# Rows scattered into the experts' lists when a block is routed, and plain loads of them in the second MoE

## The chip, the cores and the metric

The kernel runs on one core of one Trainium2 chip, as one program. Its five engines have their own instruction queues: PE (TensorE, matrix products; PEld is its weight load), DVE (VectorE), ACT (ScalarE), POOL (GpSimd) and SP (SyncE), which here only issues DMAs. The metric is the device time of one execution in microseconds (us); smaller is better. All times are of the same inputs.

## The reference

Three layers follow one another: attention over a window of 64 keys (4 batches, 8 heads, 576 positions, head size 64), a gated MLP with an RMS norm ("first MoE", 2304 tokens, 512 to 1536 to 512), and a mixture of 8 experts ("second MoE") in which each token goes to one expert:

```python
xn = x / sqrt(mean(x * x) + 1e-6) * rms_g            # first MoE
x2 = (silu(xn @ w_gate) * (xn @ w_val)) @ w_out      # (2304, 512)

logits = x2 @ wg2                                    # second MoE, 8 experts
e = argmax(logits); gw = softmax(logits)[e]
out[t] = gw[t] * (relu(x2[t] @ w1[e]) @ w2[e])       # 512 -> 1024 -> 512
```

## The kernel before, in words

The order of instructions on each engine is the order of the Python code (a manual schedule). DMAs issued by SP are plain; those issued by POOL are indirect: 128 rows go to, or come from, the DRAM rows that 128 indices name.

**First MoE.** The tokens are worked off in four blocks of 768, 768, 384 and 384 tokens, and a block of 768 in two parts of 384. A unit is one part with one of 12 slices of the hidden size; there are 72 units (loop at line 808). In a unit PE does the gate and value products (`gate_val`, line 560), ACT and DVE the activation (`silu`: a tanh on ACT at line 576, then DVE's lines 577, 578 and 580), and PE adds the output product of the unit before (`out_b`, line 597). After a part's last unit `evac` (line 603) copies its rows from PSUM into tiles `x2` and SP writes them to the DRAM tensor `x2dram` (line 614). Some work is put beside the units by a budget of VectorE time (`beside`, line 270): the norms of parts that come later (`norm`, line 308, which loads the attention's rows into a tile `xr` and squares them on ACT at line 328), the weights' conversion, and `route`.

**Routing.** `route(n)` (line 621) computes for a block's tokens the logits, the expert, the gate weight and the place `posi` in the expert's list. At line 697 POOL scatters, for each tile of 128 tokens, the pair (token number, gate weight) to row `posi` of `table` in DRAM; a memset (line 696) stands between two scatters. The last block is routed in `tail` (line 882), during the first item of the second MoE.

**Second MoE.** It has 9 items: expert 0's first 2 tiles of tokens, expert 0's next 2 tiles, then up to 4 tiles of each of the experts 1 to 7. Item 0 takes only tokens of the first two blocks, so that its list is ready early. `c_gather(i)` (line 748) loads an item's rows of `table` into a tile `ix` by SP (line 754, after all scatters so far have landed) and then gathers the tokens' rows from `x2dram` by POOL, tile by tile (line 759), into `xr` (even items) or `sq` (odd items). `c_transpose` (line 762) brings them on PE into the layout of the products, 128 tokens at a time (line 769). An item has 8 steps. The weights of all items stream through a ring of 18 places (`c_load`, line 736). `c_out` (line 938) scales an item's rows and scatters them into the output by POOL (line 944). List places that no token fills hold token number 2304, whose row of `x2dram` is zero; and when item 0 gathers, the rows of later blocks may be addressed too, so line 841 fills them from that zero row.

Lists beyond 4 tiles take a loop at the end that still reads `x2dram`; it has no turns with these inputs.

Of the kernel before, what the change touches and what calls it, by code (L numbers as in the profile page):

```python
# [23 lines left out]
E = 8  # L24
# [5 lines left out]
TINY64 = 3.4332275390625e-05  # the high word of 2.0 ** -126 as a float64, read as float32  # L30
# [3 lines left out]
# tokens of the first MoE: blocks that share a pass over the weights, in parts that share a product  # L34
BLOCKS = [[384, 384], [384, 384], [384], [384]]
SUB = 384
NXT = 3  # parts whose normed tokens are held
LEAD = 2  # steps by which the second part comes after the first at the start
MF = 1  # the last block whose tokens the second MoE's first item takes

# attention: groups of 3 query blocks from scores to transposes, to products with the values
LT, LV = 4, 5
NQK = 3  # pairs of heads whose queries and keys are held
G_LOAD, G_CONV, G_NORM = 8, 14, (12 + LV, 25 + LV)  # groups with which other work begins
CREDIT = 0.3, 0.8  # VectorE's time in us for other work beside a group: before, after the second norm's begin
BUDGET = [4.8, 3.4, 4.2, 4.2]  # the same beside a part's step, for each block
# [3 lines left out]
def attention_moe_moe_kernel(ctx, tc, qT, kT, vw, w1p, rms_g, wg2, wg2T, w2p, out):  # L50
# [13 lines left out]
    for i in range(2):  # L64
        # what the first MoE's products don't reach
        nc.vector.memset(bank[i][:, SUB:], 0.0)
# [17 lines left out]
    # places handed out so far, per partition: summed over the partitions, expert e's start at e * NT  # L84
# [4 lines left out]
    x2dram = dram.tile([NT + 1, DM], F32, name="x2dram")  # L89
    table = dram.tile([E * NT, 2], I32, name="table")  # L90
# [3 lines left out]
    # the second MoE takes over the first one's tiles  # L94
# [6 lines left out]
    # as many words are 2 steps of the first MoE and 3 of the second  # L101
# [6 lines left out]
    def xt_views(at, n):  # L108
        """Both parts of [P, 4, n] from word at on."""
        return [xt_t[:, a:a + 4 * n].rearrange("p (c t) -> p c t", c=4) for a in (at, at + 4 * n)]  # L110
# [12 lines left out]
    def parts_tiles(pl, key, n, w):  # L123
        """Places for n steps' weights in two parts, with what they hold and the step that needs it last."""
        return [[pl.tile([P, w], F32R, name=f"w{x}{key}{i}") for x in "hl"] + [None, i - n] for i in range(n)]
# [4 lines left out]
    def place(k, key, what):  # L130
        """Step k's place for the parts of what, and whether they are there."""
        p = next((p for p in places[key] if p[2] == what), None)
        here = p is not None
        if not here:
            p = min(places[key], key=lambda p: p[3])
        p[2:] = what, k
        wh_t[k, key], wl_t[k, key] = p[:2]
        return here

    # ------------------------------------------------------------------ attention  # L140
    actx = ExitStack()
    f_p = pool("fill", 1, actx)
    # additive masks on the raw scores, rows (head, query), columns keys of the window
# [17 lines left out]
    # queries of a pair of heads, [row in its block, block]; each head's rows are 0 in the other's columns  # L161
# [9 lines left out]
    def qk_load(u):  # L171
        if u < NU:
            b, hp = divmod(u, NHP)
            k_t[u] = a_q.tile([P, S], F32, name="kt")
            q_t[u] = qz[u % NQK]
            for h in range(2):
                r = slice(64 * h, 64 * h + 64)
                nc.sync.dma_start(q_t[u][r, r], qT[b, hp, r])
            # what the first scores need comes first
            cuts = [0, 192, S] if u == 0 else [0, S]  # L180
            for c in (slice(*x) for x in zip(cuts, cuts[1:])):
                nc.sync.dma_start(k_t[u][:, c], kT[b, hp, :, c])
# [66 lines left out]
    # ------------------------------------------------------------------ work beside PE's  # L249
    class Task:  # L250
        """A generator of small pieces of work. After each it gives what the piece cost VectorE in us,
        "bank" where it needs a PSUM bank until its next yield, "rest" where it would wait for another engine,
        or "step" where it would wait for longer."""
# [16 lines left out]
    def beside(tasks, budget):  # L270
        """Pieces of the tasks, the first ones first, as many as the budget allows."""
# [14 lines left out]
    def on_bank(tasks, bk):  # L286
        """The piece of the first task that asks for a bank."""
# [5 lines left out]
    # ------------------------------------------------------------------ norm of the attention's output  # L293
    # blocks of tokens that share a pass over the weights, in parts that share a product
# [13 lines left out]
    def norm(i):  # L308
        t0, nt, _ = subs[i]
        if i == 1:  # L310
            # in the place of weights that come later
# [37 lines left out]
        for _ in range(NEWTON):  # L349
            # y (the root times sc) -> y * (y * y * m / sc^2 - 3), the root times -2 * sc  # L350
# [21 lines left out]
    # ------------------------------------------------------------------ weights of the first MoE  # L372
# [3 lines left out]
    def w_load(i):  # L376
        """The i-th half of a step's weights."""
# [9 lines left out]
    def w_conv(f):  # L387
        """float64 words -> float32: sign and top exponent bit, low exponent bits and mantissa;
        what is under float32's normal range becomes 0."""
# [38 lines left out]
    # ------------------------------------------------------------------ run: attention  # L428
# [24 lines left out]
    def early_splits():  # L453
        """The first step's weights in parts."""
# [59 lines left out]
    # ------------------------------------------------------------------ first MoE  # L514
# [3 lines left out]
    def w_split(k, what, src, w_in, eng, parts="ao"):  # L518
        """Parts of float32 weights that one pass each carries: [P, w_in] for the first product(s), [P, 512]
        for the last. The second parts are left to the caller: what each costs VectorE in us, and its call."""  # L520
# [16 lines left out]
    # there and back, so that the parts at hand serve the next block too  # L537
    steps = [(n, f, list(blocks[n][2])) for n in range(len(blocks)) for f in range(NF)[::-1 if n % 2 else 1]]
    # the second part of the tokens starts later
# [43 lines left out]
    def last_mm(w, h, banks, f0, f1):  # L583
        """Adds a step's part to the output of token tiles."""
# [36 lines left out]
    def route(n):  # L621
        """Expert, weight and place in the expert's list for the tokens of block n."""
# [14 lines left out]
        if not last:  # L637
            lg = small("lg")
            for j, x2 in enumerate(x2_t.pop(n)):
# [5 lines left out]
        else:  # L645
            # on PE, in banks that nothing else needs then
# [15 lines left out]
        # the first of the largest  # L662
# [29 lines left out]
        before, now = scat[-1:], []  # L692
        for j in range(T):
            if j > 0:
                # two neighbours in an engine's order can't be declared independent
                nc.gpsimd.memset(apart, 0.0)
            d = nc.gpsimd.indirect_dma_start(out=table[:, :], in_=ent[:, j], in_offset=None,
                                             out_offset=bass.IndirectOffsetOnAxis(ap=posi[:, j], axis=0)).ins
            for o in now:
                tc.declare_no_dep(d, o, reason="other rows; the readers wait for all")  # L700
            for o in before[-1] if j == 0 and before else []:
                after(d, o)
            now.append(d)
# [12 lines left out]
    # ------------------------------------------------------------------ second MoE: parts  # L716
# [4 lines left out]
    # lists of token tiles of an expert: first expert 0's first tiles, kept to the first blocks' tokens,  # L721
    # which needn't wait for the others' routing
# [25 lines left out]
    def c_gather(i):  # L748
        if i >= len(items):
            return  # L750
        e, t0, T = items[i]
        ix = ix_t[i] = i_p.tile([P, 4, 2], I32, name="ix")
        rows = table[e * NT + t0 * P:e * NT + (t0 + T) * P]
        d = nc.sync.dma_start(ix[:, :T], rows.rearrange("(j p) w -> p j w", p=P)).ins
        for o in scat[-1]:
            after(d, o)
        xg = xg_t[i] = big(i % 2)
        for j in range(T):
            nc.gpsimd.indirect_dma_start(out=xg[:, j, :DM], out_offset=None, in_=x2dram[:, :],
                                         in_offset=bass.IndirectOffsetOnAxis(ap=ix[:, j, 0:1], axis=0))  # L760
# [13 lines left out]
    # places that expert 0's list leaves free in its first tiles  # L774
# [20 lines left out]
    # ------------------------------------------------------------------ run: first MoE  # L795
# [20 lines left out]
    for u, (k, i) in enumerate(units):  # L816
# [8 lines left out]
        # one that is free until the next step's second product  # L825
# [12 lines left out]
        if begin and n == MF:  # L838
            # rows that the first gather doesn't need, but addresses
            done = blocks[MF + 1][0]  # L840
            nc.sync.dma_start(x2dram[done:NT], x2dram[NT:NT + 1].to_broadcast([NT - done, DM]))
# [14 lines left out]
        if n == len(blocks) - 1 and last:  # L856
            # the second MoE's weights, where nothing reads the first one's any more
# [13 lines left out]
    # ------------------------------------------------------------------ second MoE  # L871
# [10 lines left out]
    def tail():  # L882
        """What follows the last block's output, up to the first list of its tokens."""
# [10 lines left out]
    def cases(i, body, unit=P // 2):  # L894
        """body(number of tokens), run by PE alone: not fewer than item i has, but for those beyond its tiles."""
# [57 lines left out]
    def over_slots():  # L953
        # what an expert has beyond 4 tiles goes into slots of 2 tiles: their expert and first table row
# [29 lines left out]
        # unused slots: within bounds  # L984
# [133 lines left out]
```

## Time and profile before

| what | us |
|---|---|
| three runs | 913.20, 912.89, 916.03 (median 913.2) |
| profiled execution, span from first to last instruction | 911.7 |
| PE busy | 852.8 (94%) |
| DVE busy | 674.6 (74%) |
| POOL busy | 253.4 (28%) |
| HBM traffic | 87.1 MB read, 19.6 MB written |

The profiled execution has no other time than its span; the median of the runs lies 1.5 us above it. Attention ends at about 135 us, the first MoE at about 621 us, and the second MoE takes the rest. In the chain of work that ended last PE has 53% of the span, DVE 26% and DMA 6%.

A row of the timeline gives the start, the duration, the engine, the line, the operation and the tiles (out<-in); in square brackets stands how long the engine was idle before it and what it waited for. A granted clock (PEclk) of 1.00 is 2.4 GHz and 0.50 is 1.2 GHz.

### The profile page before, as it was taken

The page shows a single profiled execution, that of the slowest core. Times are in us where ns is not written, and L with a number is a line of the kernel's source. Part 1 is how long each engine was busy: PE and PEld are TensorE (multiplying, and loading weights), DVE is VectorE, ACT ScalarE, POOL GpSimd, SP SyncE. Part 2 cuts the span into 40 slices and gives each one's busy share as a digit, 9 for nine tenths or more (in the row PEclk, how much of TensorE's full clock was granted, in tenths as well). Part 3 has the DMA queues.
Part 4 walks back from the last instruction along what each step waited for, and adds up shares of the span by engine and source line. Part 5 has one row for each costly group of instructions (what it writes and reads, how often), then busy time and mean ns, then how long its engine had stood idle before and what let it go on. Part 6 is the DMA issues. An engine that isn't in the chain of part 4 may idle for free.

```text
span 911.7 us, 13573 instructions
## 1 busy us (share of the span) xinstructions
PE 852.8 (94%) x4667; PEld 777.7 (85%) x4667; DVE 674.6 (74%) x1535; ACT 415.3 (46%) x951; POOL 253.4 (28%) x268
## 2 busy tenths in 40 slices
PE   8999988999999999999999899999799999899994
PEld 8999977878888999999998889888688888788883
DVE  7779989999997677776588974986485656566462
ACT  5777764334443433322333324334364545565351
POOL 3337753224323000000302243233312330333021
PEclk9999989999999999999999999999899999899998
DMA  7887623343332421000010004423376664663010
GB/s 213 286 269 241 196 86 129 104 139 104 97 112 93 139 35 35 1 1 1 17 54 1 1 1 165 171 93 83 116 215 194 210 210 122 219 209 94 3 44 17
DMA packets 40896, 102.96 MB, mean 113 GB/s; under 512 B 10576, under 2 KB 15056, under 8 KB 40659
## 3 DMA queue, kind: packets, MB, share of 16 engines
q1 hardware_dynamic: 35090, 88.29, 30.6%
q0 software_dynamic: 5696, 13.14, 5.0%
q8 instruction: 78, 1.28, 0.6%
q14 instruction: 32, 0.25, 0.1%
HBM read 87.08 MB, written 19.57 MB: 117 GB/s over the span
## 4 chain that ended last, share of the span: by engine, by line
PE 53%; DVE 26%; issue 8%; DMA 6%; ACT 4%; POOL 3%; SPq 0%; another core or an unknown queue 0%; DVEq 0%; POOLq 0%; ACTq 0%
PE bank L56 50%; DVE junk L642 6%; DMA out_dram<-x,ix 3%; DVE wla L529 3%; DVE wraw L408 2%; DVE wraw L405 2%; DVE wraw L415 2%; DVE t L578 2%; DVE t L577 2%; PE bank L769 1%; PE bank L222 1%; DVE wraw L400 1%; DVE hl L580 1%; ACT hh L579 1%; DMA sq<-x2dram,ix 1%
## 5 line engine op out<-in xcount | busy, mean ns | idle before, releaser
L56 PE MATMUL bank<-xt,wha 128*128 128x384 f32 (+3 forms) x1728 | 423.5, 330 | 20.0 <-DVE t L577 12.7
L56 PEld LDWEIGHTS bank<-xt,wha 128*128 128x128 f32 x1728 | 306.5, 191 | 39.2 <-DVE t L577 18.2
L56 PE MATMUL bank<-xt,wla 128*128 128x384 f32 (+3 forms) x864 | 283.2, 328 | 6.6 <-DVE wla L529 6.4
L56 PEld LDWEIGHTS bank<-xt,wla 128*128 128x128 f32 x864 | 164.4, 190 | 11.0 <-DVE wla L529 10.4
L56 PE MATMUL bank<-who,hl 128*128 128x512 f32 x384 | 152.8, 398 | 0.4 <-DVE hl L928 0.4
L56 PE MATMUL bank<-wlo,hh 128*128 128x512 f32 x384 | 152.5, 397 | 0.6 <-POOL wlo L529 0.6
L56 PE MATMUL bank<-who,hh 128*128 128x512 f32 x384 | 151.7, 395 | 0.6 <-issue 0.6
L579 ACT CAST hh<-t 128x384 fp32r<-128x384 f32 x72 | 37.0, 513 | 204.7 <-DVE t L578 204.7
L928 DVE SCALAR_TENSOR_TENSOR hl<-bank,hh 128x512 fp32r<-128x512 f32 (+1 forms) x72 | 45.3, 629 | 84.2 <-ACT hh L927 75.0
L529 DVE TENSOR_TENSOR wla<-wraw,wha 128x512 fp32r<-128x512 f32 (+1 forms) x112 | 98.3, 877 | 5.1 <-ACT wha L527 4.6
L642 DVE SCALAR_TENSOR_TENSOR junk<-x,wg_bc 128x512 f32<-128x512 f32 x120 | 91.3, 811 | 0.0
L56 PEld LDWEIGHTS bank<-who,hl 128*128 128x128 f32 x384 | 72.6, 189 | 18.2 <-DVE hl L928 2.1
L527 ACT CAST wha<-wraw 128x512 fp32r<-128x512 f32 (+1 forms) x113 | 87.2, 771 | 0.0
L927 ACT ACTIVATE hh<-bank 128x512 fp32r<-128x512 f32 (+1 forms) x72 | 39.7, 551 | 101.7 <-PE bank L56 86.5
L56 PEld LDWEIGHTS bank<-who,hh 128*128 128x128 f32 x384 | 72.9, 190 | 12.0 <-issue 0.8
L56 PEld LDWEIGHTS bank<-wlo,hh 128*128 128x128 f32 x384 | 72.8, 190 | 12.1 <-POOL wlo L529 0.9
L56 PE MATMUL bank<-kt,qz 128*128 128x128 f32 x288 | 76.4, 406 | 5.9 <-DMA kt<-in_kT_dram 4.5
L529 POOL TENSOR_TENSOR wlo<-wraw,who 128x512 fp32r<-128x512 f32 x30 | 48.5, 1617 | 112.2 <-ACT who L527 112.1
L56 PEld LDWEIGHTS bank<-kt,qz 128*128 128x128 f32 x288 | 72.4, 333 | 7.1 <-DVE qz L165 4.5
L527 ACT CAST who<-wraw 128x512 fp32r<-128x512 f32 x111 | 68.8, 620 | 16.8 <-PE bank L56 14.0
L208 ACT ACTIVATE wraw<-sm,nm 128x128 f32<-128x128 f32 x144 | 56.2, 391 | 30.6 <-DVE nm L204 30.3
L580 POOL TENSOR_TENSOR hl<-t,hh 128x384 fp32r<-128x384 f32 x24 | 32.9, 1372 | 113.5 <-ACT hh L579 113.5
(153 smaller groups left out, 1041.8 us busy)
## 6 DMA issues: line engine op xcount, KB each, us to landing
wraw<-in_w2p_dram SPq DMA_DIRECT2D x64, 512.0 KB, 4.6
st<-in_w1p_dram SPq DMA_DIRECT2D x24, 768.0 KB, 4.3
wraw<-in_vw_dram SPq DMA_DIRECT2D x16, 512.0 KB, 4.1
qz<-in_qT_dram SPq DMA_DIRECT2D x32, 144.0 KB, 4.8
xdram<-wraw SPq DMA_DIRECT2D x16, 288.0 KB, 2.3
x2dram<-x SPq DMA_DIRECT2D x18, 256.0 KB, 2.1
kt<-in_kT_dram SPq DMA_DIRECT2D x15, 288.0 KB, 4.6
xr<-xdram SPq DMA_DIRECT2D x4, 768.0 KB, 6.4
```

The lines of the kernel that those rows point to most:

```text
L56: nc.tensor.matmul(o, l, r, start=start, stop=stop)
L208: nc.scalar.activation(p[:, j], sm[:, j], AF.Exp, bias=nm[:, j:j + 1], scale=-1.0, accum_out=rs[:, j:j + 1])
L405: nc.vector.scalar_tensor_tensor(out=w, in0=lo, scalar=29, in1=w, op0=ALU.logical_shift_right, op1=ALU.bitwise_or)
L408: nc.vector.scalar_tensor_tensor(out=w, in0=hi, scalar=-0x40000000, in1=w, op0=ALU.bitwise_and, op1=ALU.bitwise_or)
L415: nc.vector.scalar_tensor_tensor(out=wf, in0=gt, scalar=TINY64 * TINY64, in1=wf, op0=ALU.is_ge, op1=ALU.mult)
L527: nc.scalar.copy(wh, src[:, r])
L529: e.tensor_tensor(out=wl, in0=src[:, r], in1=wh.bitcast(F32), op=ALU.subtract)))
L579: nc.scalar.copy(hh[:, :nt], t)
L580: (nc.gpsimd if subs[i][2] == 0 else nc.vector).tensor_tensor(out=hl[:, :nt], in0=t, in1=hh[:, :nt].bitcast(F32), op=ALU.subtract)
L642: nc.vector.scalar_tensor_tensor(out=junk, in0=x2, scalar=1.0, in1=wg_bc[:, e], op0=ALU.mult, op1=ALU.mult, accum_out=lg[:, j, e:e + 1])
L927: nc.scalar.activation(hh[:, :n], bank[k % 2][:, :n], AF.Relu, scale=1.0)
L928: nc.vector.scalar_tensor_tensor(out=hl[:, :n], in0=bank[k % 2][:, :n], scalar=0.0, in1=hh[:, :n].bitcast(F32), op0=ALU.max, op1=ALU.subtract)
```

## The change

A second DRAM tensor `xs` holds the experts' lists with the rows themselves. `route` scatters each tile `x2` to rows `posi` of `xs`, beside the scatter of the pair to `table`: for the first three blocks the two alternate per tile, without the memsets between; for the last block all of `xs` go first. `c_gather` then loads an item's rows from `xs` by one plain DMA on SP's queue, which waits for the scatters to `xs` alone, before the load of `ix`; the gathers are gone. The fill with zero rows is now one of `xs`, 512 rows for each expert (8 DMAs of 1 MiB, in the units 20 to 27), in place of one of 768 rows of `x2dram` after unit 23. `x2dram` is still written. Comments were taken out too, so that lines shift by up to 10.

```diff
+    xs = dram.tile([E * NT, DM], F32, name="xs")
...
-        before, now = scat[-1:], []
-        for j in range(T):
-            if j > 0:
-                # two neighbours in an engine's order can't be declared independent
+        before, now = scat[-1:], ([], [])
+        pairs = [(j, w) for j in range(T) for w in range(2)]
+        if last:
+            pairs.sort(key=lambda p: p[1])
+        at = None
+        for j, w in pairs:
+            if w == at:
                 nc.gpsimd.memset(apart, 0.0)
-            d = nc.gpsimd.indirect_dma_start(out=table[:, :], in_=ent[:, j], in_offset=None,
+            at = w
+            to, of = ((xs, x2s[j]), (table, ent[:, j]))[w]
+            d = nc.gpsimd.indirect_dma_start(out=to[:, :], in_=of, in_offset=None,
                                              out_offset=bass.IndirectOffsetOnAxis(ap=posi[:, j], axis=0)).ins
...
+        rows = slice(e * NT + t0 * P, e * NT + (t0 + T) * P)
+        xg = xg_t[i] = big(i % 2)
+        d = nc.sync.dma_start(xg[:, :T], xs[rows].rearrange("(j p) d -> p j d", p=P)).ins
+        for o in scat[-1][0]:
+            after(d, o)
         ix = ix_t[i] = i_p.tile([P, 4, 2], I32, name="ix")
-        rows = table[e * NT + t0 * P:e * NT + (t0 + T) * P]
-        d = nc.sync.dma_start(ix[:, :T], rows.rearrange("(j p) w -> p j w", p=P)).ins
-        for o in scat[-1]:
+        d = nc.sync.dma_start(ix[:, :T], table[rows].rearrange("(j p) w -> p j w", p=P)).ins
+        for o in scat[-1][1]:
             after(d, o)
-        xg = xg_t[i] = big(i % 2)
-        for j in range(T):
-            nc.gpsimd.indirect_dma_start(out=xg[:, j, :DM], out_offset=None, in_=x2dram[:, :],
-                                         in_offset=bass.IndirectOffsetOnAxis(ap=ix[:, j, 0:1], axis=0))
...
-        if begin and n == MF:
-            # rows that the first gather doesn't need, but addresses
-            done = blocks[MF + 1][0]
-            nc.sync.dma_start(x2dram[done:NT], x2dram[NT:NT + 1].to_broadcast([NT - done, DM]))
+        if 20 <= u < 20 + E:
+
+            e = u - 20
+            nc.sync.dma_start(xs[e * NT:e * NT + 4 * P], x2dram[NT:NT + 1].to_broadcast([4 * P, DM]))
```

PE's and ACT's orders stay as they were. Three places move on POOL and SP.

POOL at the end of the third block's routing, in the last unit of the first MoE; `wlo` is the low part of the weights that PE's last output product (unit 71) needs. Before:

```order
L685 TENSOR_TENSOR tot<-tot,ohb 128x8 x3
L697 DMA table<-ent,posi 18432x2
L696 MEMSET apart 128x1
L697 DMA table<-ent,posi 18432x2
L696 MEMSET apart 128x1
L697 DMA table<-ent,posi 18432x2
L529 TENSOR_TENSOR wlo_1531<-wraw_106,who_1530 128x512
```

And of the change at the same place:

```order
L688 TENSOR_TENSOR tot<-tot,ohb 128x8 x3
L707 DMA xs<-x_4839,posi 18432x512
L707 DMA table<-ent,posi 18432x2
L707 DMA xs<-x_4842,posi 18432x512
L707 DMA table<-ent,posi 18432x2
L707 DMA xs<-x_4845,posi 18432x512
L707 DMA table<-ent,posi 18432x2
L531 TENSOR_TENSOR wlo_1532<-wraw_107,who_1531 128x512
```

Three more indirect DMAs stand ahead of `wlo`.

SP from the last block's rows to the second MoE's weights; `sq` is item 1's tile and `xr` item 2's. Before:

```order
L614 DMA x2dram<-x_5500 128x512
L754 DMA ix<-table 128x2x2
L754 DMA ix<-table 128x4x2
L736 DMA wraw_111<-in_w2p_dram 128x1024 x2
L902 UNCONDITIONAL_BRANCH x2
```

And of the change:

```order
L616 DMA x2dram<-x_5510 128x512
L764 DMA sq<-xs 128x2x512
L768 DMA ix<-table 128x2x2
L764 DMA xr<-xs 128x4x512
L768 DMA ix<-table 128x4x2
L746 DMA wraw_112<-in_w2p_dram 128x1024 x2
```

The rows of item 1 are loaded ahead of its `ix`; the six gathers that POOL issued after the two loads of `ix` are gone.

SP around the end of the first block (units 20 to 28); `xr<-xdram` are loads for norms of later parts. Before:

```order
L851 DMA wg_bc<-in_wg2T_dram 128x4096
L319 DMA xr<-xdram_96 128x4x192
L319 DMA xr<-xdram_97 128x4x192
L614 DMA x2dram<-x_2826 128x512
L614 DMA x2dram<-x_2829 128x512
L614 DMA x2dram<-x_2832 128x512
L614 DMA x2dram<-x_2880 128x512
L614 DMA x2dram<-x_2883 128x512
L614 DMA x2dram<-x_2886 128x512
L841 DMA x2dram<-x2dram 768x512
L319 DMA xr<-xdram_97 128x4x384
```

And of the change, from the first row of the first part on:

```order
L616 DMA x2dram<-x_2830 128x512
L616 DMA x2dram<-x_2833 128x512
L616 DMA x2dram<-x_2836 128x512
L851 DMA xs<-x2dram 512x512
L616 DMA x2dram<-x_2885 128x512
L616 DMA x2dram<-x_2888 128x512
L616 DMA x2dram<-x_2891 128x512
L851 DMA xs<-x2dram 512x512 x4
L321 DMA xr<-xdram_97 128x4x384
```

One fill stands between the two parts' rows, and four stand ahead of the last part's load in place of one.

## Rows read from the trace of the kernel before

**Rows 1.** The page's first part: busy time, share of the span, instructions.
```profile
PE 852.8 (94%) x4667; PEld 777.7 (85%) x4667; DVE 674.6 (74%) x1535; ACT 415.3 (46%) x951; POOL 253.4 (28%) x268
```

**Rows 2.** Waits of PE from 640 us on: total, times, longest.
```profile
PE bank L769 <- DMA sq<-x2dram,ix: 5.7, 2, 4.1
PE bank L56 <- issue: 4.6, 3, 3.5
```

**Rows 3.** Timeline of PE around item 1's first transposes.
```profile
645.68 0.39 PE L56 MATMUL bank<-who,hl 128*128 128x512 f32 x1
647.60 0.66 PE L769 MATMUL bank<-ident,sq 128*128 128x128 f32 x4 [1.53 <-DMA sq<-x2dram,ix]
652.38 1.12 PE L769 MATMUL bank<-ident,sq 128*128 128x128 f32 x4 [4.12 <-DMA sq<-x2dram,ix]
```

**Rows 4.** Busy time by stretch, then granted clock, DMA share, GB/s.
```profile
651.10:657.70 6.60, 5.32 (x19) 4.74 (x20) 0.69 (x1) 0.59 (x1) 0.00 (x0) 0.50 0.48 169
...
792.10:797.70 5.60, 5.60 (x20) 4.91 (x21) 1.29 (x2) 1.19 (x3) 0.00 (x0) 0.50 0.26 92
```

**Rows 5.** Chain of waits into item 1, start and us of each piece.
```profile
636.99 3.83 DMA table<-ent,posi
...
641.39 1.94 DMA ix<-table
...
645.10 7.24 DMA sq<-x2dram,ix
```

**Rows 6.** The page's sixth part: DMA issues, KB each, median us to landing.
```profile
wraw<-in_w2p_dram SPq DMA_DIRECT2D x64, 512.0 KB, 4.6
...
x2dram<-x SPq DMA_DIRECT2D x18, 256.0 KB, 2.1
...
xr<-xdram SPq DMA_DIRECT2D x4, 768.0 KB, 6.4
```

**Rows 7.** Timeline of POOL at the third block's scatters.
```profile
614.03 1.37 POOL L697 DMA_INDIRECT table<-ent,posi  x1 [2.96 <-DVE posi L690]
...
618.17 1.30 POOL L529 TENSOR_TENSOR wlo<-wraw,who 128x512 fp32r<-128x512 f32 x1
```

**Rows 8.** Timeline of PE in the last output product.
```profile
618.51 0.39 PE L56 MATMUL bank<-who,hh 128*128 128x512 f32 x1
619.52 0.50 PE L56 MATMUL bank<-wlo,hh 128*128 128x512 f32 x1 [0.62 <-POOL wlo L529]
```

**Rows 9.** Indirect DMAs of 2-KB rows into the output: count, ns min/median/max.
```profile
L944 POOL DMA_INDIRECT out_dram<-x,ix x32: 977/997/1497, 659.6 to 903.1; - x32
```

**Rows 10.** Timeline of SP, the first block's rows and the fill.
```profile
302.13 8.46 SPq L614 DMA_DIRECT2D x2dram<-x  x6
310.63 0.54 SPq L841 DMA_DIRECT2D x2dram<-x2dram  x1
341.62 0.37 SPq L319 DMA_DIRECT2D xr<-xdram  x1
```

**Rows 11.** Columns as in rows 4: a stretch in which the fill runs alone.
```profile
314.00:324.00 10.00, 9.70 (x51) 9.04 (x52) 8.30 (x20) 3.80 (x7) 0.00 (x0) 1.00 0.82 125
```

**Rows 12.** Timeline of ACT at the last norm's squares.
```profile
346.46 1.76 ACT L328 ACTIVATE sq<-xr 128x384 f32<-128x384 f32 x4
348.69 0.49 ACT L576 ACTIVATE t<-bank 128x384 f32<-128x384 f32 x1 [0.46 <-PE bank L56]
```

**Rows 13.** Timeline of DVE and of PE: the activation, the next gate product.
```profile
349.70 0.55 DVE L577 SCALAR_TENSOR_TENSOR t<-t,bank 128x384 f32<-128x384 f32 x1
...
352.65 0.51 PE L56 MATMUL bank<-xt,wha 128*128 128x384 f32 x2
```

**Rows 14.** Timeline of POOL at the second block's scatters, first and sixth.
```profile
539.42 1.01 POOL L697 DMA_INDIRECT table<-ent,posi  x1 [2.11 <-DVE endb L780]
...
546.33 0.96 POOL L697 DMA_INDIRECT table<-ent,posi  x1 [0.19 <-issue]
```

**Rows 15.** Timeline of PE at item 0's first transposes.
```profile
561.12 0.60 PE L769 MATMUL bank<-ident,xr 128*128 128x128 f32 x4
```

**Rows 16.** Timeline of PE after its second long stop.
```profile
792.09 0.80 PE L56 MATMUL bank<-xt,wha 128*128 128x256 f32 x2 [3.48 <-issue]
```

More of the change, by code (lines that the diff above doesn't have):

```diff
@@ L638, in route @@
             lg = small("lg")
-            for j, x2 in enumerate(x2_t.pop(n)):
+            x2s = x2_t.pop(n)
+            for j, x2 in enumerate(x2s):
                 for e in range(E):
@@ L691, in route @@
         yield 0.9
-        before, now = scat[-1:], []
-        for j in range(T):
-            if j > 0:
+        before, now = scat[-1:], ([], [])
[5 more added lines that the diff above has]
+            if w == at:
                 nc.gpsimd.memset(apart, 0.0)
-            d = nc.gpsimd.indirect_dma_start(out=table[:, :], in_=ent[:, j], in_offset=None,
+            at = w
+            to, of = ((xs, x2s[j]), (table, ent[:, j]))[w]
+            d = nc.gpsimd.indirect_dma_start(out=to[:, :], in_=of, in_offset=None,
                                              out_offset=bass.IndirectOffsetOnAxis(ap=posi[:, j], axis=0)).ins
-            for o in now:
+            for o in now[w]:
                 tc.declare_no_dep(d, o, reason="other rows; the readers wait for all")
-            for o in before[-1] if j == 0 and before else []:
+            for o in before[-1][w] if not now[w] and before else []:
                 after(d, o)
-            now.append(d)
+            now[w].append(d)
             if not last:
```

## The prediction

> **What bounds the kernel now.** I read the busy times first, then PE's waits by stretch, then the granted clock, then the timeline of the engines that release PE. The reader is to see that PE is busy for 94% of the span [rows 1], so that time can only come from its few stops or be lost by new ones. After 640 us PE waits for two things that count: the gathered rows of item 1, 5.7 us in two stops of 1.53 and 4.12 us, and once "issue", 3.48 us, for which the profile has no releaser [rows 2, 3, 16]. Behind either long stop PE runs at a granted clock of 0.50 (1.2 GHz) for a while: its work of 5.32 and of 5.60 us there would take half of that at 1.00, so each long stop costs 2.7 to 2.8 us more than its length [rows 4]. The change is aimed at the first stop. The other terms are stops that it may make.
>
> **A. The stop before item 1 (gain).** The chain into it: the last scatter to `table` starts on POOL at 636.99 and lands 3.83 us later; SP loads `ix`, 1.94 us after its issue; POOL then gathers, and the second gather takes 7.24 us, beside four gathers for item 2 and a load of weights [rows 5]. In the change POOL issues the three scatters to `xs` at the same places in time. The third thus starts at 636.99 and I give it 4.2 us (3.83 and some for 256 KB in place of 1 KB): 641.2. SP then issues a load of 512 KB with nothing ahead of it in its queue; loads of that size land 4.6 us after their issue [rows 6]: 645.9. PE comes to the transposes at 646.07, the end of the row at 645.68 [rows 3]. So they no longer wait for DMA, or by some tenths. What is late next are the casts of the transposed tiles, by which PE then waits for ACT and DVE: I leave 1.0 us of the 5.65. The clock doesn't fall: 2.7 us. Gain 7.35, taken as 7.4. Behind the first load on SP stand the load of `ix` (needed only by item 1's output), the 1-MiB load of item 2, and the weights; SP waits there for the scatters to `table`, now three DMAs later, some 4 us. The weights fill places of an 18-deep ring and are not due soon, and item 2's rows are due some 8 us after item 1's products begin: no cost. Bounds: 8.4 (all 5.65 and the clock), and 0, if the chain is as late as now (a loss only if it is later).
>
> **B. The last output product (loss).** The third block's scatters stand on POOL ahead of `wlo`, for which PE already waits by 0.62 us [rows 7, 8]. Three scatters took POOL from 614.03 to 618.17. In the change six stand there. Indirect DMAs of 2-KB rows take POOL 1.0 us each, as those of pairs do [rows 9]; from one scatter to the next it is 6.91 / 5 = 1.38 us with a memset between [rows 14], and 1.3 without. The three more cost 3 x 1.3 = 3.9 us. `wlo` then ends at 623.4 in place of 619.5, and PE stands for 0.62 + 3.9 = 4.5 us. Nothing covers this: PE takes its instructions in order, and the last block's routing, which is behind that product, shifts with it, so A doesn't get shorter by it. The stop is as long as the two behind which the clock fell, so I add 2.8: 6.7 us. Bounds: 2.9 (three times 0.977, and no fall of the clock) and 3 x 1.8 + 2.8 = 8.2 (three at the longest of rows 9 with their gaps).
>
> The Trainium skill says on its page "SBUF — State Buffer" (SBUF: two separate sides) that descriptor generation for POOL's DMAs is starved while VectorE runs certain two-port operations. The spread of rows 9, 977 to 1497 ns, would fit it; if it held here at every one of the added DMAs, B would be 1.5 us more, within the bound above.
>
> **C. Item 0's rows (loss).** Before, SP loaded `ix` and POOL gathered ahead of the third block's rows; now the load stands behind six scatters to `xs` and six to `table`. The last to `xs` is the eleventh: 539.42 [rows 14] + 10 x 1.3 = 552.4. Plus 4.2 to land and 4.6 for 512 KB, as in A: 561.2. PE comes to the transposes at 561.12 [rows 15]: a wait of 0 to 1, taken as 0.3. Bounds: 0, and 3 with the scatters at the longest of rows 9.
>
> **D. The fills (loss).** This term decides. The fill of 1.57 MB runs at 125 GB/s when alone [rows 11], so 1 MiB takes 8.4 us. SP's DMAs run in order of issue: the fill of 310.63 moves nothing until the rows issued before it are through. The fills of units 20 to 22 fall where the queue is empty, and cost nothing. The one of unit 23 is issued behind the first three rows' writes of 302.13 [rows 10], starts at about 306 and ends at 314.4; the next three writes take 2.1 [rows 6], to 316.5; the four fills of units 24 to 27 then take 33.6, to 350.1. Behind them stands the load of the last part's rows, issued at 341.62; it had landed by 346.46 at the latest, when ACT's squares began without waiting [rows 10, 12], so it takes 4.8 at most: 350.1 + 4.6 = 354.7. ACT takes its instructions in order: the four squares (1.76 us) and the tanh behind them (0.49) then end at 357.0 where they ended at 349.18, and DVE's line 577 (0.55) reads the tanh and frees the bank: 357.6. PE comes to the next gate product at 352.65 [rows 13]. So it stands for 5.0 us, and the clock falls behind it, 2.7: 7.7 us. PE can stand a load that lands up to 349.8; each us later costs one. Bounds: 0, if the fills overlap so that the load lands by then, and 12, if they run at 110 GB/s (4.4 us later).
>
> The Trainium skill, "DMA: Bandwidth & Descriptors" (Queues, rings and completion order), says that each DMA engine consumes one queue's descriptors in ring order. The rows bear that out for the fill of 310.63, and no row shows a load behind several fills; if it did not hold, D would be 0.
>
> **Not on the path.** The later items' loads leave POOL for SP; PE waits for none of these gathers now [rows 2]. The 18 scatters more and 32 gathers fewer shift POOL's busy time, which has room [rows 1]. An `x2` tile is now held until its scatter lands; of the 8 places the one that is wanted soonest is that of the second block's first scatter, by one copy on ACT, and the tanh behind it has some slack: nothing.
>
> **Sum.** -7.4 + 6.7 + 0.3 + 7.7 = +7.3 on the span of 911.7: 919.0. The median of the runs lies 1.5 above that span, so 920.5.
>
> **Rivals.**
> 1. The fills are hidden (D = 0): they run faster side by side than one alone, or the load gets in between. For it: no row shows more than one fill at a time. Against: one fill alone kept the DMA engines 82% busy [rows 11]. Sum -0.4: 912.8, no change.
> 2. Faster: the fills are hidden and the stop of 3.48 us at 792.09, with its clock, doesn't come back, because the gathers that crowd DMA there are gone. It is worth 3.5 + 2.8 = 6.3. For it: the stop has no releaser but falls in a crowd of transfers. Against: the bytes per item stay the same. Sum -6.7: 906.5. With D as forecast it gives 914.2, no change.
> 3. Slower still: the chain into item 1 stays as late as it is. The place is the load of `sq` in the tail; it decides if the three scatters and the load need over 6 us more than I give them, so that rows land after 652. A is 0: +14.7, 927.9. Against: DMA is idle at that time but for them.
> 4. The change doesn't do what it says, and PE still waits for the `table`: the order shows the load of rows ahead of `ix`, so I give it no chance of its own.
>
> **How the numbers follow.** Forecast (B and D both cost, A gains) 0.48; rival 1 0.20; rival 2 0.22, of which 0.07 with the fills hidden; rival 3 0.10. The measurement can tell 0.5%, 4.6 us: faster is under 908.6, slower over 917.8. Faster: 0.07 and 0.03 of rival 1 = 0.10. Same: 0.17 of rival 1, 0.14 of rival 2 and 0.06 of the forecast at small D = 0.37. Slower: 0.42 of the forecast, 0.01 of rival 2 and 0.10 = 0.53. The forecast's own range is 916 to 925 (D 3 to 12); the range over the cases is 908 to 927: it leaves out the fastest case and the end of the slowest.
>
> **What would show it.** D: in the profile after, ACT's squares at line 330 wait for `xr<-xdram` at about 346 us, and PE for line 579 at about 353. B: PE waits some 4 us for POOL's `wlo` in the last output product, with a PEclk of 0.5 behind it. A: no wait for `sq` before item 1's transposes, and no 0.5 there. C: under 1 us before item 0's. The prediction is wrong if PE has no stop near 353, or if the one for `sq` is still there.

## The result, and the profile after

| kernel | median, us | runs | ratio to before, 95% interval |
|---|---|---|---|
| before | 912.89 | 7, 907.84 to 917.02 | 1 |
| changed | 921.17 | 7, 918.37 to 924.27 | 1.0107 [1.0080, 1.0134] |

The changed kernel is slower. The medians lie 8.3 us apart, where 7.3 were forecast on the span: 921.2, where 920.5 was forecast. The ratio, which isn't that of the two medians (1.0091), would make it 9.8. The profiled execution took 918.37 with a span of 916.6. It is the fastest of the seven, and the two traces differ by 4.9 us in span and not by 8.3.

PE does the same work in the same order up to 640 us, so the shift of one product against its own start in the trace before measures a term without any sum. Each shift below is such a difference. First the waits of PE (us in total, times, longest), from 340 to 640 us and then from 640 us on; at the top a row of ten short waits for `wla` is left out, 6.5 us in total, 6.4 before:

```profile
...
PE bank L56 <- DVE t L579: 5.2, 1, 5.2
PE bank L56 <- POOL wlo L531: 4.5, 1, 4.5
PE bank L779 <- DMA xr<-xs: 1.5, 1, 1.5
...
PE bank L56 <- ACT who L529: 4.0, 2, 2.1
PE bank L56 <- issue: 3.9, 4, 2.2
PE bank L56 <- ACT xt L781: 1.0, 1, 1.0
```

The first two rows here are terms D and B, the third is C. The row for `sq` of [rows 2] has no successor: A's stops are gone, and so is the stop of 3.48 us of [rows 16].

**D.** The chain into the stop (start, us), then PE at the stop and after it, and from the trace before the product that answers to 364.32:

```profile
341.67 13.58 DMA xr<-xdram
...
355.70 1.33 ACT sq L330 x3
357.04 0.38 ACT t L578
...
357.44 0.57 DVE t L579
```

```profile
358.05 1.01 PE L56 MATMUL bank<-xt,wha 128*128 128x384 f32 x2 [5.18 <-DVE t L579]
...
364.32 0.34 PE L56 MATMUL bank<-xt,wla 128*128 128x384 f32 x1
```

```profile
356.14 0.33 PE L56 MATMUL bank<-xt,wla 128*128 128x384 f32 x1
```

The load issued at 341.67 lands at 355.25, ACT's squares and tanh follow, and PE stands for 5.18 us. Its shift is 358.05 - 352.65 = 5.4 [rows 13] at the stop and 364.32 - 356.14 = 8.2 behind the slow clock, which thus took 2.8.

**The granted clock** in four stretches (columns as in rows 4: busy times, then granted clock, DMA share, GB/s):

```profile
357.10:364.00 6.90, 5.95 (x19) 5.95 (x20) 5.46 (x12) 1.83 (x4) 0.00 (x0) 0.51 0.00 0
633.60:637.00 3.40, 3.40 (x11) 2.72 (x10) 0.69 (x1) 0.89 (x2) 0.00 (x0) 0.50 0.83 40
646.50:658.00 11.50, 11.50 (x78) 10.31 (x78) 8.20 (x24) 6.05 (x13) 7.90 (x13) 1.00 0.29 72
722.40:725.80 3.40, 3.40 (x12) 2.82 (x11) 1.29 (x2) 1.18 (x3) 1.84 (x2) 0.50 0.74 230
```

Behind D the clock is at 0.50 (1.2 GHz) for 6.9 us, much as in [rows 4], but behind B for 3.4 us only. Before item 1 it stays at 1.00. The fourth stretch is new, behind a stop that nobody had foreseen.

**B.** POOL at the third block's scatters (the first, the sixth, then `wlo`), and PE:

```profile
623.83 1.35 POOL L707 DMA_INDIRECT xs<-x,posi  x1 [2.96 <-DVE posi L693]
...
630.89 0.96 POOL L707 DMA_INDIRECT table<-ent,posi  x1 [0.30 <-issue]
631.88 1.27 POOL L531 TENSOR_TENSOR wlo<-wraw,who 128x512 fp32r<-128x512 f32 x1
```

```profile
633.20 0.50 PE L56 MATMUL bank<-wlo,hh 128*128 128x512 f32 x1 [4.48 <-POOL wlo L531]
```

From the first scatter to `wlo` it is 631.88 - 623.83 = 8.05 us, where [rows 7] had 4.14. The stop is 4.48 us; 4.5 was forecast. The shift is 633.20 - 619.52 = 13.7 there [rows 8], and 15.2 once the clock is back, by these products after and before:

```profile
637.31 0.28 PE L56 MATMUL bank<-xt,wla 128*128 128x256 f32 x1
```

```profile
622.06 0.28 PE L56 MATMUL bank<-xt,wla 128*128 128x256 f32 x1
```

**C.** The chain into item 0's rows, start and us: the last scatter to `xs`, the load, the transposes.

```profile
560.89 4.17 DMA xs<-x,posi
...
565.22 5.71 DMA xr<-xs
...
570.97 0.66 PE bank L779 x4
```

The shift there is 570.97 - 561.12 = 9.85 [rows 15], and 9.9 behind the transposes: 1.7 more than behind D, of which PE's wait for the load is 1.45.

**A.** POOL, SP and PE in the tail: the third scatter to `xs`, the load of item 1's rows, the transposes, and a product behind them; then the same product before.

```profile
652.37 1.25 POOL L707 DMA_INDIRECT xs<-x,posi  x1 [0.19 <-issue]
```

```profile
655.43 0.37 SPq L764 DMA_DIRECT2D sq<-xs  x1
```

```profile
661.14 0.62 PE L779 MATMUL bank<-ident,sq 128*128 128x128 f32 x4
...
665.00 0.40 PE L56 MATMUL bank<-xt,wha 128*128 128x256 f32 x2
```

```profile
657.78 0.31 PE L56 MATMUL bank<-xt,wha 128*128 128x256 f32 x1
```

The load lands at 661.05 and PE starts at 661.14 without a wait. The shift, 15.2 us behind B, falls to 665.00 - 657.78 = 7.2.

**The second MoE.** From there to PE's end the shift goes from 7.2 to 6.0, but not quietly. (Behind PE's last product the rest of the program is 1.1 us shorter than before, 11.6 for 12.7 us; hence the 4.9 of the spans.) How much this stage takes varies: from the same product on the shift changes by +3.1 us in the trace of `e1_fills_later`, +6.1 in `e2_wlo_first`, -4.3 in `e3_both` and +2.7 in `e5_rows_first`, none of which edits that stage. PE's stops over 0.9 us there were 3.48 and 1.04; now they are 2.06, 1.98, 1.14, 0.97 and 2.18, most at the change from one item to the next. The view of the DMA queues shows what these stops share with the one that had no releaser. First the changed kernel, 712.3 to 718.6 us and 718.6 to 721.2, then the kernel before, 782.4 to 789.1 and 789.1 to 792.1 (queue, kind: packets, MB, share of 16 engines):

```profile
q1 hardware_dynamic: 595, 1.45, 69.9%
...
q1 hardware_dynamic: 743, 0.63, 74.3%
q0 software_dynamic: 25, 0.10, 10.0%
q8 instruction: 1, 0.02, 2.5%
```

```profile
q0 software_dynamic: 272, 0.91, 54.7%
q1 hardware_dynamic: 270, 1.00, 39.2%
...
q1 hardware_dynamic: 168, 0.61, 60.0%
q0 software_dynamic: 181, 0.32, 28.0%
q8 instruction: 1, 0.02, 2.0%
```

Queue q8 brings instructions, in this stage mostly a packet of 16 KB every 3 to 6 us. In the first stretch of either kernel it brings none for 6.3 or 6.7 us, while loads or gathers fill the DMA engines; then one comes, and PE goes on. From that packet's start to PE's next product it is 2.4 us (718.7 to 721.14, PE's row: `[2.06 <-ACT who L529]`) and 2.9 us (789.2 to 792.09 [rows 16]). In the changed kernel's other four: 2.5 (781.9 to 784.47), 2.3 (808.0 to 810.29), 2.9 (817.9 to 820.80) and 2.9 (826.9 to 829.76). Three kernels of the experiments have it too: 710.1 to 712.48 and 802.9 to 805.33 in `e2_wlo_first`, 705.2 to 707.60 in `e3_both`, 797.1 to 799.39 in `e5_rows_first`. A long gap on q8 is not always a stop: from 676.9 to 685.3 us there is one of 8.4 and PE goes on.

The trace also holds what PE does until then. In `cases` (line 912) PE's sequencer tests an expert's count of tokens, by compare-branches, to choose for how many tokens the products are made. First all of that line's in the changed kernel, then the one ahead of the stop at 721.14 (ns min/median/max, first and last start):

```profile
L912 PEldq COMPARE_BRANCH  x201: 70/208/4522, 661.2 to 903.9; - x101
```

```profile
L912 PEldq COMPARE_BRANCH  x1: 4522/4522/4522, 716.6 to 716.6; - x1
```

It ends at 721.09, 0.06 us ahead of PE's product, while the cast on ACT that the waits view names had ended at 720.83. 26 of these branches take over 0.6 us, and each of them ends 2.3 to 3.3 us after the start of a packet on q8. Most are hidden behind products that PE has in hand. Four of the five stops, and the one of 3.48 us before, end 0.06 us behind a compare-branch: a long one, or a short one right behind a long one. The fifth (810.29) has only the packet. So in these stops, "issue" and waits put down to ACT alike, PE waits for instructions. That the crowd of transfers is what makes a packet late is argued from the first stretches above.

### The profile page after: what moved, and what is told of

Its sections match the earlier page's. It is cut to its first block, busy times and chain, and to the rows that moved or that the text cites. A ratio compares the mean times of both kernels' runs of the same rounds, so it can differ in the third digit from the quotient of the medians.

```text
span 916.6 us, 13572 instructions
## 1 busy us (share of the span) xinstructions
PE 851.7 (93%) x4667; PEld 777.4 (85%) x4667; DVE 675.2 (74%) x1535; ACT 416.2 (45%) x951; POOL 237.6 (26%) x244
## 4 chain that ended last, share of the span: by engine, by line
PE 49%; DVE 26%; issue 11%; DMA 6%; ACT 3%; POOL 3%; SPq 0%; POOLq 0%; DVEq 0%; ACTq 0%
PE bank L56 46%; DVE junk L645 6%; DMA out_dram<-x,ix 3%; DVE wraw L410 2%; DVE wla L531 2%; DVE wraw L407 2%; DVE t L580 2%; DMA xr<-xdram 2%; DVE t L579 2%; DVE wraw L417 2%; DVE wraw L402 2%; PE bank L224 1%; PE bank L779 1%; DVE hl L582 1%; ACT hh L581 1%
## 5 line engine op out<-in xcount | busy, mean ns | idle before, releaser
L954 POOL DMA_INDIRECT out_dram<-x,ix x32 | 34.4, 1074 | 217.2 <-ACT x L953 210.2
L529 ACT CAST wha<-wraw 128x512 fp32r<-128x512 f32 (+1 forms) x113 | 87.1, 771 | 0.0
L529 ACT CAST who<-wraw 128x512 fp32r<-128x512 f32 x111 | 68.8, 620 | 17.7 <-PE bank L56 17.5
```

Of the source, the lines that this page charges most:

```text
L529: nc.scalar.copy(wh, src[:, r])
L954: d = nc.gpsimd.indirect_dma_start(out=out[:, :], in_=y, in_offset=None, out_offset=bass.IndirectOffsetOnAxis(ap=ix[:, j, 0:1], axis=0), b ...
```

## Experiments

Each was timed against the kernel before on the chip that it ran on; a difference of two ratios can join two chips. It is turned into us with 912.6 and is uncertain by about 3.5 us (two intervals of 0.0027). By the medians the prices of D and B below are 7.5 and 7.7 in place of 9.6 and 9.1.

| run | median, us | ratio, 95% interval |
|---|---|---|
| e1_fills_later | 913.08 | 1.0002 [0.9979, 1.0026] |
| e2_wlo_first | 912.87 | 1.0007 [0.9982, 1.0031] |
| e3_both | 904.18 | 0.9922 [0.9893, 0.9950] |
| e4_fills_alone | 928.87 | 1.0190 [1.0159, 1.0222] |
| e5_rows_first | 903.71 | 0.9899 [0.9874, 0.9924] |
| e6_rows_spread | 903.85 | 0.9895 [0.9868, 0.9922] |
| e7_gather_item1 | 920.58 | 1.0077 [1.0047, 1.0107] |
| e8_all | 899.47 | 0.9861 [0.9833, 0.9890] |
| e9_table_first | 915.74 | 1.0024 [0.9998, 1.0049] |

### e1_fills_later: term D taken away

```diff
-        if 20 <= u < 20 + E:
-            e = u - 20
+        if 20 <= u < 24 or 34 <= u < 38:
+            e = u - 20 if u < 24 else u - 30
```

> The changed kernel with the fills of experts 4 to 7 issued at units 34 to 37, behind the load of the last part's rows, in place of units 24 to 27. Theory (the load waits in SP's queue behind the fills): the stop before line 579 at 353 us (5.2 us) and the 0.50 clock behind it are gone, together 8.2 us by the shift of PE's products against before; ACT's squares no longer wait for xr<-xdram; 921.2 - 8.2 = 913.0. Rival 1 (the load is late for another reason, for example the DRAM tile xs itself): the stop stays, 921. Rival 2 (the fills only move their price to a later stage): the stop goes, another of several us comes after 370 us, 917 to 921.

913.1, as the theory has it; by the ratios D is 0.0105, 9.6 us. ACT's squares have no wait (its row in the trace):

```profile
345.15 1.76 ACT L330 ACTIVATE sq<-xr 128x384 f32<-128x384 f32 x4
```

Rival 1 falls: PE has no stop at 353, and none over 0.4 us between there and 500 us. Rival 2 falls at the size that it gave, but a part of D comes back at item 0:

```profile
PE bank L779 <- DMA xr<-xs: 2.7, 1, 2.7
```

Behind this stop the clock is at 0.50 for 3.4 us, and C takes 4.5 us by the shift (-1.3 to 3.2) in place of 1.7. In the five kernels with the later fills and the same order of scatters (e1, e3, e6, e7, e9) the stop is 2.1 to 3.1 us, in the two with the early fills 1.5 and 0.6; why is open. In this trace B's stop is 4.48 us again, but behind it the clock stays low twice as long as in the changed kernel:

```profile
625.50:632.30 6.80, 5.83 (x19) 5.07 (x20) 1.57 (x3) 2.21 (x4) 1.22 (x4) 0.50 0.68 148
```

### e2_wlo_first: term B taken away

```diff
         rest = b_split(heads[u + 1], "o") if u + 1 in heads else []
+        if u == len(units) - 2:
+            for _, r in rest:
+                r()
+            rest = []
```

> The changed kernel with POOL's last wlo issued ahead of the third block's six scatters in place of behind them. Theory: PE's stop of 4.48 us before the last output product goes wholly and the 0.50 clock behind it too; by the shift of PE's products 3.8 + 1.4 = 5.2, and up to 0.6 more, since before stood there for 0.62: 915.4 to 916.0. The last block's routing follows that product and comes earlier by as much, so item 1's rows still land in time. Rival: the scatters themselves are late by one wlo and the tail with them, or PE waits for another engine there: under 2 us are won, 919 to 921.

912.9: 9.1 us by the ratios (7.7 by the medians), more than the 5.2 to 5.8 expected, at the edge of what the intervals allow. `wlo` now stands ahead of the first scatter on POOL, and PE's waits from 600 to 640 us hold nothing of POOL, only the row of the second fence:

```profile
619.54 1.29 POOL L531 TENSOR_TENSOR wlo<-wraw,who 128x512 fp32r<-128x512 f32 x1 [2.22 <-ACT who L529]
621.14 1.24 POOL L707 DMA_INDIRECT xs<-x,posi  x1 [0.30 <-DVE posi L693]
```

```profile
PE bank L56 <- DVE wla L531: 1.5, 2, 1.0
```

By the shift, which falls by 0.9 us here where it rose by 5.3, the place gives 6.2; the rest of the surplus is not shown. The traced execution (915.74) is longer than the median: D's stop, untouched by the edit, is 3.82 us and not 5.18, since the last fill landed at 351.75 and not 353.30, but the second MoE loses 6.1 us, in four stops for instructions. Both prices thus differ from one execution to the next.

### e3_both: the two together

> Both edits. Theory (the terms add): 921.2 - 8.2 - 5.2 to -5.8 = 907.2 to 907.8, and 5 us under the kernel before. Rival (part of either gain comes back as stops in the second MoE): 909 to 913.

904.2, 3 us under the range of the theory: 16.9 us by the ratios, against 9.6 + 9.1. The two add, within their uncertainty, and the kernel is 0.8% faster than before. The two spans differ by 17.2 us (916.6 to 899.4), by the shifts 8.3 of D and 6.3 of B, less 0.7 at item 0, and 3.1 in the second MoE, where the granted clock is 1.00 over the whole stretch in spite of three stops of 1.7 to 2.3 us. Those 3.1 are of one pair of executions, and this stage varies by more.

```profile
640.00:890.00 250.00, 238.97 (x1395) 210.48 (x1393) 157.81 (x267) 135.03 (x243) 36.54 (x37) 1.00 0.46 151
```

### e4_fills_alone: the kernel before with the eight fills

```diff
+        if 20 <= u < 20 + E:
+            e = u - 20
+            nc.sync.dma_start(xs[e * NT:e * NT + 4 * P], x2dram[NT:NT + 1].to_broadcast([4 * P, DM]))
         if begin and n == MF:
             done = blocks[MF + 1][0]
```

> The kernel before with the eight fills of units 20 to 27 added, into a DRAM tile that nothing reads; all else as before, its own fill of x2dram too (so nine fills). Theory: the whole term D alone: a stop of over 5 us at 353 and the clock, 912.9 + 8.2 = 921.1, more by up to 8 if the ninth fill (1.57 MB) also stands ahead of the load. Rival (the stop needs the rest of the change): 913.

928.9: with the fill of `x2dram`, which stays, nine fills alone cost more than the whole change, 17.3 us. ACT's squares and PE's stop:

```profile
367.45 1.76 ACT L329 ACTIVATE sq<-xr 128x384 f32<-128x384 f32 x4 [21.00 <-DMA xr<-xdram]
```

```profile
370.22 1.01 PE L56 MATMUL bank<-xt,wha 128*128 128x384 f32 x2 [17.51 <-DVE t L578]
```

The stop is 17.51 - 5.18 = 12.3 us longer for 1.57 MB more: 128 GB/s, near the 125 of [rows 11], where the expectation gave that fill up to 8 us. So a byte of fill ahead of the load costs PE its time in the queue, one for one.

### e5_rows_first: term C taken away, from e3_both

```diff
-        if last:
+        if last or n == MF:
             pairs.sort(key=lambda p: p[1])
```

> The kernel with both edits (904.2), and the second block's six scatters to xs ahead of its six to the table, as the last block's are. Theory (item 0's rows are late because the last scatter to xs is the eleventh on POOL): the load is issued some 5 us earlier and PE's stop before item 0's transposes (1.5 in the changed kernel, 2.1 in the kernel with both edits) is gone: 902 to 903. Rival (the stop is set by the load's own 5.7 us or by another engine): 904.

The load is issued at 550.44 and PE has no stop before item 0's transposes. Start and us of the transposes' row, which has no bracket:

```profile
562.36 0.60 PE L779 MATMUL bank<-ident,xr 128*128 128x128 f32 x4
```

So the place is as the theory has it. The time, 903.7 against 904.2, is too close to tell: 2.1 us by the ratios, uncertain by more than that.

### e6_rows_spread: the later items' loads in four pieces, from e3_both

```diff
         if f in (2, 3, 4, 5):
+            c_rows(i + 2, slice(f - 2, f - 1))
             c_transpose(i + 1, f - 2, bank[2 + f % 2])
         if f == 6:
-            c_gather(i + 2)
+            c_gather(i + 2, False)
```

(`c_rows` issues the load of some tiles' rows; `c_gather` with False then loads only `ix`.)

> The kernel with both edits (904.2), and the 1-MiB load of each later item's rows cut into four loads of 256 KB, issued one to a step. Theory (PE's stops behind the items' changes, 2.3, 1.7, 0.7 and 1.8 us in the kernel with both edits, come from its instruction fetches, which are late while the 1-MiB load and a load of weights crowd the DMA engines): no two fetches lie over 6 us apart around an item's change there, the stops fall under 0.7 each, 898 to 901. Rival (they are the waits for ACT's two copies at an item's change, to which the waits view puts some): the stops stay, 904.

The time isn't as expected, and the mechanism is so in part. Between 673 and 821 us `e3_both` has four gaps over 5.9 us between the starts of q8's packets: three of 6.4 to 7.5 ahead of stops of 2.26, 1.72 and 0.65 us, and one of 6.9 with no stop behind it. Here the three are gone and the fourth is left (740.1 to 747.0); the stops of 1.7 to 2.3 us are gone. But PE waits from 640 us on read:

```profile
PE bank L56 <- ACT xt L791: 4.0, 4, 1.2
PE bank L56 <- issue: 2.8, 6, 1.1
PE bank L789 <- DMA sq<-xs: 1.9, 1, 1.9
```

0.8 to 1.2 us each now goes at five places, four of them put down to ACT's casts of the transposed rows, and in this execution item 1's rows were late by 1.9. All four end 0.06 us behind a compare-branch and 2.9 to 3.1 us after the start of a packet on q8; in three of them the cast had ended 0.3 to 0.5 us before, so these at least are waits for instructions too. 27 of PE's branches take over 0.6 us here, the longest 3.5, where `e3_both` has 20 and one of 4.7: more and shorter ones. 903.9 against 904.2: nothing that can be measured. Nor do the pieces always help: `e8_all` has them, and its trace has a stop of 2.94 us behind a gap of 6.8 on q8 (769.9 to 776.6):

```profile
779.62 0.50 PE L56 MATMUL bank<-xt,wha 128*128 128x256 f32 x2 [2.94 <-issue]
```

That late instructions make these stops is shown by the branches; that cutting the load cures them, or pays, is not.

### e7_gather_item1 and e9_table_first: term A undone, from e3_both

```diff
 # e7: item 1 alone through the table
+        if i == 1:
+            for j in range(T):
+                nc.gpsimd.indirect_dma_start(out=xg[:, j, :DM], out_offset=None, in_=x2dram[:, :],
+                                             in_offset=bass.IndirectOffsetOnAxis(ap=ix[:, j, 0:1], axis=0))
 # e9: e7, and in the last block the table's scatters first
-            pairs.sort(key=lambda p: p[1])
+            pairs.sort(key=lambda p: -p[1])
```

> The kernel with both edits (904.2), but item 1's rows gathered by POOL through the table, as before. Theory (term A, the products' shift from 15.1 to 7.2 us between the traces of before and after): the two stops for sq and the 0.50 clock are back, + 7.9 = 912.1, about the kernel before. Rival (with the fills and wlo out of the way the tail is early enough anyway): under + 3, 907 at most.

> As the kernel that gathers item 1's rows through the table (920.6), but in the last block the three scatters to the table stand ahead of the three to xs on POOL, so that the chain into item 1 is the one of the kernel before. Theory (9.73 us of stop there are the 5.65 of before and some 4 us for three scatters to xs that stand ahead of the table's): the stop falls to 5.7 us or a little over (item 1's gathers now stand behind three scatters to xs, which may add up to 2), 914 to 917, and term A by it is 10 to 13 with the stops in the second MoE that follow. Rival (the gathers themselves are slower now, since nothing of the chain but the order changed): the stop stays over 9, 920.

920.6, and 915.7. e7 lies 8.5 us over its theory, for it was badly put: it kept the three scatters to `xs` ahead of the table's, so its chain is longer than the one before and its 14.1 us (by the ratios) aren't A's. e9 puts that right. PE's waits for item 1's rows in e7 and in e9:

```profile
PE bank L784 <- DMA sq<-x2dram,ix: 9.7, 1, 9.7
```

```profile
PE bank L784 <- DMA sq<-x2dram,ix: 6.5, 2, 3.8
```

Three scatters at the head of POOL's queue are worth 9.7 - 6.5 = 3.2 us of stop. With the old order the stop is 6.5, near the 5.65 of before, and A is 0.0102, 9.3 us, under the 10 to 13 expected. A stretch of 10.2 us at 0.50 (6.6 in [rows 4]) is in it: by the shift e9 loses 1.5 us at item 1 against the kernel before, which aren't the change's.

### e8_all: all four edits

> All four edits: fills later, wlo first, rows first, loads spread. If the terms add: 904.2 - 1.5 - 4 = 898.7, from 896 to 901. If only the first two edits count: 904.

899.5, 1.4% faster than before: the best version. Its interval ends at 0.9890, below that of e3_both, but it overlaps those of e5_rows_first and e6_rows_spread, so which of the last two edits does it is open. It lies within 896 to 901, but the sum behind that range has 4 us for the loads in pieces, which e6 doesn't show: that it came so near 898.7 is luck in part.

## Why the prediction was right, point by point

The sum was +7.3 on the span; the shifts make it +7.2 at 665 us and +6.0 at PE's end, and the span of the trace grew by 4.9. The median came within 0.7 us of the forecast, nearer than the terms deserve: C was 1.4 too low and B 1.4 too high, and the second MoE, taken as 0, moves by several us from one trace to the next. The directions, the places and the chains are what the prediction earned; the closeness of the total is in part luck. The terms (the last column from runs that take one away, each uncertain by 3.5):

| term | foreseen | shift in the trace | by runs |
|---|---|---|---|
| D, the fills | +7.7 | 5.4 + 2.8 = +8.2 | +9.6 |
| C, item 0's rows | +0.3 | 9.9 - 8.2 = +1.7 | +2.1, not resolved |
| B, `wlo` | +6.7 | 3.8 + 1.5 = +5.3 | +9.1 |
| A, the stop for `sq` | -7.4 | 7.2 - 15.2 = -8.0 | -9.3 |
| second MoE | 0 | -1.2 | |

- **D was right in place, chain and size**: squares waiting for `xr<-xdram`, PE for line 579, 5.18 us where 5.0 was foreseen, with 2.8 for the clock where 2.7 was. Two of its pieces were off and cancelled. The last fill landed at 353.30 and not 350.1: that of unit 23 landed at 316.57 and not 314.4, and the last four 8.2 to 9.3 us apart where 8.4 was reckoned. The load landed 1.95 us behind it and not 4.6. Rival 1 is refuted by e1 and e4. The rule of the Trainium skill that the prediction weighed ("DMA: Bandwidth & Descriptors", Queues, rings and completion order), that a DMA engine consumes one queue's descriptors in ring order, holds here: 1.57 MB more in the queue ahead of the load made the stop 12.3 us longer (e4).
- **B's stop was right to 0.02 us; its clock was not.** 2.8 was added because the stop was as long as those of [rows 4]. The trace has 3.4 us at 0.50, worth 1.5; e1 has 6.8 us behind the same stop. Only the size of the clock's part failed, and it varies. By the rule of the Trainium skill ("SBUF — State Buffer", SBUF: two separate sides) that some of VectorE's operations starve the descriptor generation of POOL's DMAs, the added scatters could have been 1.5 us dearer, an estimate of the prediction. The trace doesn't show that here: the three more took 3.9 us in all, as reckoned without it.
- **C was mis-sized.** The scatters went as foreseen (13.2 us from the first to the last to `xs`, foreseen 13.0; 4.2 to land), but the load took 5.71 and not 4.6, and that is 1.1 of the missing 1.4 us. The bounds of 0 to 3 held it here, but not in every trace: the stop was 3.1 us in e6, and in e1 it cost 4.5 us with the clock behind it, for which C had no term.
- **A was right**, with 0.6 too little: no wait for ACT's casts is left, where 1.0 was allowed. It has no slack, though: the load took 5.6 us, not 4.6, and landed 0.09 us ahead of PE, and in e6 it came 1.9 late.
- **"Not on the path" was half right.** PE waits for none of the later items' loads, but it still stops for late instructions while they run. Rival 2 foresaw the loss of the 3.48 us stop and got it; its gain of 6.3 didn't come, because five smaller stops of the same kind, 8.3 us together, took its place. The step that failed there is that with the gathers the crowd would be gone: the 1-MiB load fills the DMA engines in the same place (69.9% of them in the stretch shown).
- Rival 3 is refuted by the trace: nothing of the `sq` stop is left.

So the change wins 8 to 9 us at item 1, and loses 13.5 (by the shifts) to 19 (by the runs) in two queues that it lengthens, SP's and POOL's. With both put right it is faster than before.

## What to carry to other kernels

When work moves to another queue, list what stands behind each new entry and when that is due: here fills and scatters cost more in the queues than the removed gathers gave, and moving them by a few positions turned 1.1% slower into 0.8% faster. Bulk fills belong behind the last load that somebody waits for, and a short operation that PE waits for belongs ahead of a row of indirect DMAs. To undo one part of a change for a test, look at the order of the whole chain again: e7 measured a chain that neither kernel had. And before a wait is believed, compare the end of the releaser that is named with the start of what waited: 0.3 us and more between them meant here that a branch, which the waits view doesn't name, came last.

## What the runs showed of the hardware that was not expected

- A compare-branch of PE's sequencer takes 0.21 us in the median and up to 4.52 in the changed kernel's second MoE; the 26 over 0.6 us end 2.3 to 3.3 us after the start of an instruction packet on q8. One of 4.4 or 4.5 us left PE standing for 2.0 or 2.1, and the waits view may name ACT.
- A stop of the same 4.48 us had a clock of 0.50 for 3.4 us behind it in one trace and for 6.8 us in another; one of 2.7 us at item 0 had 3.4 us in e1 and 6.8 in e7, and stops of 2.1 and 2.3 us in e3_both and of 3.1 in e6 had none. The clock behind a stop of this size is a range, not a figure.
- Four fills of 1 MiB, one behind the other in one queue, landed 8.2 to 9.3 us apart in one execution, and the stop that they cause was 5.18 us in one trace and 3.82 in another.
